# Weights in pieces of 4, 4 and 8 column tiles, and the order of every engine from tables

## The chip, the cores and the metric

The kernel runs on one core of a Trainium2 chip. The metric is the device time of one execution in microseconds; lower is better. PE is the matrix engine (TensorE), with PEld for its weight loads; ACT is ScalarE, DVE is VectorE, POOL is GpSimd, SP is SyncE.

## The reference, cut to what matters

```python
def _attn_ref(q, k, v, alpha):            # (4, 8, 768, 48) each
    B, H, S, D = q.shape
    state = np.zeros((B, H, D, D))
    for t in range(S):
        state = alpha[:, :, t, :, None] * state + np.einsum('bhd,bhe->bhde', k[:, :, t], v[:, :, t])
        y[:, :, t] = np.einsum('bhd,bhde->bhe', q[:, :, t], state)
    return y

def _moe_ref(x, w_in, w_out):             # x (3072, 384), w_in (384, 2048), w_out (2048, 384)
    r = np.maximum(x @ w_in, 0.0)
    return (r * r) @ w_out
```

The rows of x are the outputs of the first part, all heads side by side. It is a linear attention with a decay for each channel, followed by a dense layer, a squared ReLU and a second dense layer.

## The kernel before, in words

**Tiles.** The 3072 tokens are cut into 12 tiles (`units`) of 256: three stretches of the sequence for each of four batches. Tile g has two tokens in a partition. Tiles 0 to 3 are the first stretch of each batch, so the state of one batch is needed again four tiles later.

**Attention of tile g** (the numbers are names of operations, given by `name=` in `add`): loads `lda`, `ldk`, `ldq`, `ldv`; the product of two neighbouring decays `pr` and its logarithm `ln`; matmuls with a triangle of ones for the cumulative sums, `m1i` and `m1s`; exponentials `ei`, `ea`, `ec`, `es`; scaled keys and queries `ekm`, `eqm` into QKS; transposes `tr` into KQT (on PE with copies `et` out of PSUM for tiles 0 to 2, as DMA transposes on SP's queue from tile 3 on); scores `p`, masked on DVE into PM (`mk0`, `mk1`); v in bf16 (`vc`); the state's matmuls `kv` with `sa`, `sc`, `sd` behind them; the output `y`, copied by `xe` and transposed by `xt` (PE with a copy `xv` for tiles 0 to 3, DMA from tile 4 on). Tile 0 is worked in two halves of heads, so its names have the half in them (`ln0_0`, `ekm1_0`).

**Dense layers of tile g.** The first layer is eight units `s1_g_u` of 6 matmuls, each into one of two PSUM banks in turn. Each is emptied by a ReLU `re` (ACT or DVE); squares `sq` of one or two units follow (DVE, ACT or POOL). The second layer is eight units `s2_g_j_sg` of 4 matmuls into one bank, emptied by `oe`, stored by `out`; the last half tile has a form of its own (`last_tile`, L980).

**Weights.** W_in and W_out are loaded on POOL's queue, which turns fp32 into bf16, in two halves of 8 column tiles each. `hidden` says which columns of W_in make up tile `fj`, `weight` loads a piece, and a unit waits for the piece that it reads.

**Order.** `Program.add` records an operation with what it reads and writes, the engines that could do it, costs and a priority. `Program.schedule` replays the whole list against a model of engines and DMA rings and so gives each engine its queue; `MOVED` and `CHOSEN` shift priorities and fix engines for some names. `fill` puts dummy matmuls (L1104) into PE's gaps before the first dense unit. `place` derives the waits, `emit` writes each queue out. From then on each engine works strictly in the order of its queue: an operation that waits holds all behind it, and a DMA's issue waits in its engine's queue like any other instruction. `AFTER` ties some loads to the landing of others: tile 2's loads to W_in's first piece, W_out's first piece to W_in's second, tile 3's loads to W_out's first piece.

Of the kernel before, what the change touches and what calls it, by code (L numbers as in the profile page):

```python
# [2 lines left out]

# [11 lines left out]
class Op:  # L15


    __slots__ = ("alts", "eng", "fn", "cost", "prio", "deps", "idx", "lag", "sem", "start", "end", "pos", "name",
                 "users", "ndeps", "mode", "ready", "land", "pace")

    def __init__(self, alts, prio, name):
        self.alts, self.prio, self.name = alts, prio, name
        self.eng = self.fn = self.cost = None
        self.deps = {}
        self.lag = 0
        self.sem = None
        self.users = []
        self.pace = ()
        self.pos = None
        self.mode = ("F", "F")  # L30
        self.ready = 0.0
        self.start = self.end = self.land = None


class Program:
# [3 lines left out]
    HOP = 35  # L39
    PE_LATENCY = 170  # L40
    DMA_FIRST = {"sp": 1300, "act": 1300, "pool": 2000}
    PACKET = (("win", 172), ("wout", 490), ("ld", 22), ("tr", 18), ("xt", 18), ("out", 125))
    SBUF_ONLY = ("pr", "bk", "aq", "ekm", "eqm", "sq", "sb", "sd")
    BIAS = {"pool": 300}
    DMA_LAST = 800
    SWITCH = 95
    HALVED = {"qks": 3, "kqt": 3, "raw": 3, "ek": 3, "eq": 3, "acm": 2, "laf": 2}
    AFFINITY = 2500
    MOVED = {
# [6 lines left out]
    }  # L56
    CHOSEN = {
# [4 lines left out]
    }  # L62

    def __init__(self, nc):
        self.nc = nc
        self.ops = []
        self.writer = {}
        self.readers = {}
        self.dma_sems = {}
        self.dma_count = {}  # L70
        self.filler = None

    def add(self, eng, fn, cost, prio, reads=(), writes=(), name="", dma=None, lag=0, after=(), mode=("F", "F"),
# [7 lines left out]
        if name in self.CHOSEN:  # L81
            choices = {self.CHOSEN[name]: choices[self.CHOSEN[name]]}
        op = Op(choices, prio + self.MOVED.get(name, 0), name)
# [3 lines left out]
        if dma is not None:  # L87
            if dma not in self.dma_sems:
                self.dma_sems[dma] = self.nc.alloc_semaphore("d_" + dma)
                self.dma_count[dma] = 0  # L90
            self.dma_count[dma] += 1
            op.sem = (dma, self.dma_count[dma])
# [25 lines left out]
    def schedule(self):  # L118

        for op in self.ops:  # L120
            op.ndeps = len(op.deps)
            for d in op.deps:
                d.users.append(op)
        engines = sorted({e for op in self.ops for e in op.alts})
        free = {e: 0.0 for e in engines}
        shared = {"dve": 0.0, "pool": 0.0}
        mode = "F"
        rings = {"sp": [], "act": [], "pool": []}
        left = {}
        clock = [0.0, 0]  # L130
        events = []
        seq = itertools.count()

        def push(t, kind, what):
            heapq.heappush(events, (t, next(seq), kind, what))

        def rates():
            took = {r: next(t for n, t in self.PACKET if q[0].name.startswith(n)) for r, q in rings.items() if q}
            return {r: t / sum(took.values()) for r, t in took.items()}

        def advance(t):
            rate = rates()
            for r, q in rings.items():
                if q:
                    left[q[0]] -= rate[r] * (t - clock[0])
            clock[0] = t
            for r, q in rings.items():
                while q and left[q[0]] <= 1e-6:
                    op = q.pop(0)
                    land(op, t + self.DMA_LAST)  # L150
            clock[1] += 1
            rate = rates()
            nxt = [left[q[0]] / rate[r] for r, q in rings.items() if q]
            if nxt:
                push(t + min(nxt), "tick", clock[1])

        def land(op, t):
            op.land = t
            for u in op.users:
                u.ndeps -= 1  # L160
                e = op.eng
                if op.sem is None and e == "pe" and "pe" in u.alts:
                    ready = op.end
                elif u.deps[op] or e not in u.alts:
                    ready = t + self.HOP
                else:
                    ready = op.end
                u.ready = max(u.ready, ready)
                if u.ndeps == 0:
                    push(max(u.ready, now), "ready", u)  # L170

        now = 0.0
        for op in self.ops:
            if op.ndeps == 0:
                push(0.0, "ready", op)
        avail = {e: [] for e in engines}
        order = {e: [] for e in engines}
        while events:
            now = events[0][0]
            while events and events[0][0] <= now + 1e-9:  # L180
                _, _, kind, op = heapq.heappop(events)
                if kind == "tick":
                    if op == clock[1]:
                        advance(now)
                elif kind == "arrive":
                    advance(now)
                    rings[op.eng].append(op)
                    left[op] = op.lag
                    advance(now)
                elif kind == "ready":  # L190
                    best = None
                    for e, (_, c) in op.alts.items():
                        t = max(now, free[e]) + c + self.BIAS.get(e, 0)
                        t += sum(o.alts[e][1] for o in avail[e] if (o.prio, o.idx) < (op.prio, op.idx))
                        if best is None or t < best[0]:
                            best = (t, e)
# [33 lines left out]
    def fill(self, make, sizes, until, after, cold):  # L230
# [5 lines left out]
        for o in self.order["pe"]:  # L236
            while t < until:
                slow = 2 if t < cold else 1
                fits = [(n, c) for n, c, gap in sizes if o.start - t > gap + (slow - 1) * c]
                if not fits:  # L240
                    break
# [120 lines left out]
def bass_gla_recurrent__then__act_relu_squared_kernel(  # L362
# [29 lines left out]
    WS = 2  # L392
# [744 lines left out]
```

## Time and profile before

| | |
|---|---|
| median of 3 runs | 175.64 us (174.52 to 177.49) |
| the profiled execution | 175.72 us, span 174.0 us |
| busy of the span | PE 97%, DVE 68%, ACT 69%, POOL 14% |
| first layer's matmuls (L1010) | 73.7 us busy, 576 |
| second layer's matmuls (L1050) | 68.9 us busy, 368 |
| DMA | 33.36 MB, mean 192 GB/s |

How to read it: the page names an engine, a line of the kernel and the tiles, out<-in, with the number of instructions. A row of a timeline has the start in the span, the time, the engine, line and operation, and in brackets how long the engine had been idle and what ended that. A row of the waits has the waiting engine and line, what it waited for, the total in us, how often, and the longest. A row of windows has, for each engine, busy time and instructions in a stretch, in the order PE, PEld, DVE, ACT, POOL, then PE's granted clock, the DMA share and GB/s. Matmuls overlap each other in the records, so a row's time is longer than what it adds to the next one's start.

### The profile page before, as it was taken

The numbers are of one execution on the slowest core, as the hardware profiler recorded it, in microseconds if no ns is written. First come the engines' busy times: TensorE is split into PE (matmuls) and PEld (weight loads), VectorE is DVE, ScalarE is ACT, GpSimd is POOL, SyncE is SP. The second block draws the span as 40 slices with busy tenths as digits, with TensorE's granted clock in tenths as the row PEclk, the third lists the DMA queues.
The fourth block names the chain that finished last, engine by engine and source line by source line (L and its number), as shares of the span: only waits on it lengthen the run. The fifth ranks groups of instructions, "written<-read, shape, count | busy, mean of one in ns | idle before, by whom it ended". The sixth has DMA issues, their size and how long they took to land.

```text
span 174.0 us, 5086 instructions
## 1 busy us (share of the span) xinstructions
PE 168.1 (97%) x2234; PEld 130.0 (75%) x2234; DVE 119.1 (68%) x194; ACT 119.6 (69%) x214; POOL 24.0 (14%) x32
## 2 busy tenths in 40 slices
PE   7999998999999989999999999999999999999994
PEld 2556877866878767777778777878788697688773
DVE  5479569789878679984958948948949727332230
ACT  4848768877758399697878849759668564566440
POOL 3920961010224124200000000000000000000000
PEclk9999999999999999999999999999999999999999
DMA  5999999999998997999999998989999590040022
GB/s 145 351 288 210 259 281 212 259 284 280 191 215 188 245 207 97 340 194 238 283 185 196 269 176 191 261 182 221 234 191 190 95 184 4 0 136 4 13 79 90
DMA packets 71030, 33.36 MB, mean 192 GB/s; under 512 B 67552, under 2 KB 67808, under 8 KB 71008
## 3 DMA queue, kind: packets, MB, share of 16 engines
q1 hardware_dynamic: 69024, 26.75, 68.9%
q0 software_dynamic: 1984, 6.29, 14.9%
q8 instruction: 17, 0.28, 0.6%
q14 instruction: 5, 0.04, 0.1%
HBM read 25.17 MB, written 4.72 MB: 172 GB/s over the span
## 4 chain that ended last, share of the span: by engine, by line
PE 78%; DMA 14%; POOL 3%; ACT 2%; DVE 1%; issue 1%; SPq 1%
PE psWH L1010 33%; PE psO L1050 33%; DMA win<-in_moe_w_in_dram 5%; DMA raw<-in_alpha_dram 5%; DMA raw<-in_v_dram 4%; POOL raw L535 2%; PE psX L811 2%; PE psZ L779 2%; PE psX L908 2%; PE psX L800 2%; PE psX L980 2%; PE psZ L908 1%; PE psWH L652 1%; ACT rr L1018 1%; POOL prd L645 1%
## 5 line engine op out<-in xcount | busy, mean ns | idle before, releaser
L1010 PE MATMUL psWH<-xt,win 128*128 128x256 bf16 x576 | 73.7, 275 | 1.8 <-DVE xt L966 1.0
L1010 PEld LDWEIGHTS psWH<-xt,win 128*128 128x128 bf16 x576 | 65.3, 145 | 6.9 <-ACT rr L1018 1.3
L1050 PE MATMUL psO<-wout,gt 128*128 128x384 bf16 x368 | 68.9, 326 | 0.0
L1018 ACT ACTIVATE rr<-psWH 128x512 bf16<-128x512 f32 x85 | 50.3, 596 | 20.5 <-PE psWH L1010 18.7
L1050 PEld LDWEIGHTS psO<-wout,gt 128*128 128x128 bf16 x368 | 34.8, 98 | 18.4 <-DVE gt L1028 0.2
L1028 DVE TENSOR_TENSOR gt<-rr 128x1024 bf16<-128x1024 bf16 (+1 forms) x39 | 23.7, 610 | 24.5 <-ACT rr L1018 24.5
L919 DVE TENSOR_TENSOR pm<-psZ,caus 128x1024 bf16<-128x1024 f32 x12 | 14.6, 1218 | 2.3 <-PE psZ L908 2.3
L919 DVE TENSOR_TENSOR pm<-psX,caus 128x1024 bf16<-128x1024 f32 x12 | 14.6, 1219 | 1.5 <-PE psZ L908 1.5
L1032 ACT ACTIVATE gt<-rr 128x1024 bf16<-128x1024 bf16 (+1 forms) x18 | 15.2, 843 | 0.4
L939 ACT ACTIVATE xbf<-psX 128x768 bf16<-128x768 f32 x11 | 8.9, 810 | 8.2 <-PE psX L800 7.4
L1057 ACT ACTIVATE osb<-psO 128x384 f32<-128x384 f32 x17 | 8.4, 491 | 5.9 <-PE psO L1050 5.4
L1104 PE MATMUL psO<-zero 128*128 128x512 bf16 (+1 forms) x34 | 10.3, 432 | 1.3 <-DVE zero L455 1.3
L714 DVE TENSOR_TENSOR qks<-raw,eq 128x384 bf16<-128x384 f32 x18 | 9.4, 552 | 2.0 <-DMA raw<-in_q_dram 1.8
L719 DVE TENSOR_TENSOR qks<-raw,ek 128x768 bf16<-128x768 f32 x11 | 10.5, 951 | 0.1
L710 ACT ACTIVATE vbf<-raw 128x768 bf16<-128x768 f32 x9 | 7.5, 837 | 3.7 <-DMA raw<-in_v_dram 3.7
L1020 DVE TENSOR_SCALAR rr<-psWH 128x512 bf16<-128x512 f32 x11 | 7.6, 688 | 0.6
L646 ACT ACTIVATE lab<-prd 128x384 bf16<-128x384 f32 x10 | 5.2, 520 | 3.5 <-DVE prd L643 2.5
L874 DVE TENSOR_TENSOR smd<-psZ,sbd 128x384 bf16<-128x384 f32 x8 | 4.4, 556 | 4.4 <-PE psX L800 4.4
L672 DVE TENSOR_TENSOR ek<-ek,raw 128x384 f32<-128x384 f32 x9 | 6.3, 705 | 1.4 <-ACT ek L663 1.4
L645 POOL TENSOR_TENSOR prd<-raw 128x384 f32<-128x384 f32 x4 | 4.1, 1036 | 19.0 <-DMA raw<-in_alpha_dram 19.0
L1104 PEld LDWEIGHTS psO<-zero 128*128 128x128 bf16 x34 | 3.2, 109 | 4.5 <-issue 1.9
L1059 DVE COPY osb<-psO 128x384 f32<-128x384 f32 x6 | 3.3, 557 | 4.6 <-PE psO L1050 4.6
(118 smaller groups left out, 170.6 us busy)
## 6 DMA issues: line engine op xcount, KB each, us to landing
out_dram<-osb SPq DMA_DIRECT2D x11, 384.0 KB, 4.3
raw<-in_alpha_dram SPq DMA_DIRECT2D x10, 384.0 KB, 5.2
raw<-in_k_dram SPq DMA_DIRECT2D x10, 384.0 KB, 5.6
raw<-in_q_dram SPq DMA_DIRECT2D x10, 384.0 KB, 3.9
raw<-in_v_dram SPq DMA_DIRECT2D x10, 384.0 KB, 4.5
win<-in_moe_w_in_dram POOLq DMA_DIRECT2D x2, 768.0 KB, 10.3
wout<-in_moe_w_out_dram POOLq DMA_DIRECT2D x2, 768.0 KB, 8.9
raw<-in_alpha_dram POOLq DMA_DIRECT2D x2, 384.0 KB, 4.9
```

What stands on the lines that cost most here:

```text
L714: add("dve", lambda e, j=j, dst=dst: e.tensor_tensor(dst, RAW[r][:, 2, :, j, :].rearrange("p (n x) d -> p n x d", x=2), EQ[la][:, j].rearr ...
L719: add("dve", lambda e, a=a, E=E: e.tensor_tensor(QKS[qs][:, a, :, :, 0:D], RAW[r][:, 1 + a].rearrange("p h j d -> p j h d"), E[la][:].rear ...
L919: add("dve", lambda e, hf=hf, psT=psT: e.tensor_tensor(PM[pm][:, hf].rearrange("p r n j t -> p (r n) (j t)"), psT[:, :, :].rearrange("p r ...
L939: add("act", lambda e: e.activation(XBF[x2][:], psX[:, :, 0:HD], AF.Copy), act_ns(2 * HD), p0 + 6100, reads=[("ps", "X", 0), ("ps", "X", 1 ...
L1010: ins = pe.matmul(psH[hb][:, i * T:(i + 1) * T], WIN[:, kk, hidden(fj)], mov, start=(kk == 0), stop=(kk == KT - 1))
L1018: add("act", lambda e, hb=hb, rr=rr: e.activation(rr, psH[hb], AF.Relu), act_ns(512), pu + 600, reads=[("ps", "H", hb)], writes=[("rr", rb ...
L1020: alts={"dve": (lambda e, hb=hb, rr=rr: e.tensor_scalar(rr, psH[hb], 0.0, None, ALU.max), dve_ns(512))})
L1028: add("dve", lambda e, dst=dst, sq=sq: e.tensor_tensor(dst, sq, sq, ALU.mult), 148 + k * 267, pu + 1200, reads=[("rr", rb, h) for h in ran ...
L1032: "act": (lambda e, dst=dst, sq=sq: e.activation(dst, sq, AF.Square), act_ns(k * 512))})
L1050: ins = pe.matmul(psS, GT[gt][:, fj, j, :], WOUT[:, fj, :], start=(fj == 0), stop=(fj == FT - 1))
L1057: add("act", lambda e, j=j, psS=psS: e.activation(OSB[ob][:, j], psS, AF.Copy), act_ns(DM), ps_ + 700, reads=[keyS], writes=[("osb", ob, j ...
L1104: pr.fill(lambda n: lambda pe: pe.matmul(psO[:, 0:n], ZERO[:, 0:128], ZERO[:, 0:n], skip_group_check=True), ((512, 216, 420), (256, 109, 2 ...
```

## The change

The search inside the kernel goes; what it decided is replaced by five tables of names, one for each engine, in which `~512` and `~256` are dummy matmuls of that width. `schedule` reads them, gives each operation the engine whose table names it, and counts the DMA semaphores by queue. Dependences and waits are derived as before.

```diff
-    def schedule(self):
...
-    def fill(self, make, sizes, until, after, cold):
-    def unpace(self):
+    def schedule(self, tables, filler):
+        named = {o.name: o for o in self.ops}
+        queues = {}
+        for e, text in tables.items():
+            queues[e] = []
+            for word in text.split():
+                if word[0] == "~":
+                    ...
+                else:
+                    o = named.pop(word)
+                o.eng = e
+                o.fn, o.cost = o.alts[e]
+                o.pos = len(queues[e])
+                queues[e].append(o)
...
-    WS = 2
-    FS = FT // WS
+    PIECES = ((0, 4), (4, 4), (8, 8))
+    def piece(fj):
+        return max(w for w, (at, n) in enumerate(PIECES) if at <= fj)
     def hidden(fj):
-        w, e = divmod(fj, FS)
-        return slice(w * FS * 128 + e, (w + 1) * FS * 128, FS)
+        at, n = PIECES[piece(fj)]
+        return slice(at * 128 + fj - at, (at + n) * 128, n)
...
-            add("pe", s1, ..., reads=[("xt", s)] + sorted({("win", f // FS) for f in fjs}), ...
+            add("pe", s1, ..., reads=[("xt", s)] + sorted({("win", piece(f)) for f in fjs}), ...
-                    ... + [("wout", sg * WS // 4)],
+                    ... + [("wout", piece(sg * FT // 4))],
```

Further branches that come with it (`SPLIT_X`, `SPLIT_KV`, `HALF_LOADS`, `WIDE`) are empty or off. The starts of the tables:

```
pe:   ~512 x8 m11_0 m10_0 ~512 ~512 ~512 ~512 ~512 ~256 ~256 tr00_0 ~512 ~256 kv0
      tr01_0 ~256 ~256 tr10_0 ~512 ~512 ~256 tr11_0 p0_0 ~256 ~256 p1_0 m11 ~512 ~512 ~512 ~512 y0 ~512 ~512 ~512
      ~512 xt0 tr0_1 ~256 ~256 s1_0_1 tr1_1 s1_0_0 s1_0_3 p0_1 s1_0_2 s1_0_5 s1_0_4 kv1 m1i2 s1_0_7 y1 s1_0_6 xt1
      m1s2 tr0_2 s1_1_1 s1_1_0 s1_1_3 s1_1_2 s2_0_0_0 tr1_2 s1_1_5 s1_1_4 p0_2 s2_0_0_1 s1_1_6 s2_0_0_2 s2_0_0_3 ...
act:  table ln1_0 ln0_0 ei1_0 ei0_0 ea1_0 ea0_0 vc0 ec0_0 ln1 copycaus ec1_0 ei1 ea1 ec1 xe0 et1_1 re0_3 re0_2 vc1
      re0_5 ln2 re0_4 ei2 re0_7 xe1 ea2 ec2 es2 re1_1 re1_0 re1_3 sq1_1 vc2 re1_6 re1_5 oe0_0 ln3 ...
dve:  ... ekm1_0 ekm0_0 zcaus et00_0 eqm1_0 zlaf1 eqm0_0 zlab1 et01_0 et10_0 sa0 et11_0 mk0_0 mk1_0 sc0 zlab0 ekm1
      eqm1 xv0 et0_1 re0_1 re0_0 mk0_1 mk1_1 pr2 sd0 sq0_3 sa1 zqks2 sc1 bk2 ekm2 xv1 re0_6 ...
pool: slinc slstr scaus1 sident lda1 ldk1 ldq1 win0 scaus win1 win2 ldv1 lda2 ldk2 wout0 ldq2 sq0_1 ldv2 wout1
      wout2 sd1 sq0_5 sq1_3 sq0_7 sq0_6 vc3 pr4 pr6 bk5 sq3_1 sq3_5 sd4 sq3_7 ...
sp:   lda0 ldv0 ldk0 ldq0 lda3 ldv3 ldk3 lda4 lda5 ldq3 ldq4 ldk4 lda6 tr0_3 tr1_3 ldv4 ldk5 ldq5 tr1_4 tr0_4
      out0_1 ldv5 ldk6 ldv6 tr0_5 tr1_5 xt4 lda7 ...
```

By engine, the tables give 63 ReLUs to ACT and 33 to DVE (85 and 11 before); 22 squares to DVE, 18 to ACT and 20 to POOL (39, 18 and 3 before); the products `bk` and `pr` and the states `sd` to POOL in 13 cases instead of 6; and the copies `xe` to DVE in 4 cases instead of 1. Both kernels have 34 dummy matmuls, all before the first dense unit.

More of the change, by code (lines that the diff above doesn't have):

```diff
@@ L230, in fill @@
-    def fill(self, make, sizes, until, after, cold):
-        new = []
-        t = after.land + self.HOP
-        cold += t
[L236 to L241, printed above, removed]
-                n, c = fits[0]
-                f = Op({"pe": (make(n), c)}, 0, "fill")
-                f.idx = len(self.ops)
-                f.eng, f.fn, f.cost = "pe", make(n), c
-                f.start, f.end = t, t + c * slow
-                f.deps = {after: True}
-                self.ops.append(f)
-                new.append(f)
-                t = f.end
-            new.append(o)
-            t = max(t, o.end)
-        for i, o in enumerate(new):
-            o.pos = i
-        self.order["pe"] = new
```

358 lines of the change are left out of this document (169 added, 189 removed), and 10 rows, old and new, of tables (CHOSEN, MOVED).

## The prediction

> **What bounds the kernel now.** I read the page first, then the matrix engine's waits, then its timeline at the two places where it waited, then the timelines of the engines that it waited for.
>
> ```profile
> span 174.0 us, 5086 instructions
> PE 168.1 (97%) x2234; PEld 130.0 (75%) x2234; DVE 119.1 (68%) x194; ACT 119.6 (69%) x214; POOL 24.0 (14%) x32
> PEclk9999999999999999999999999999999999999999
> PE psO L1104 <- DVE zero L455: 1.3, 1, 1.3
> PE psWH L1010 <- DVE xt L966: 1.0, 1, 1.0
> PE psWH L1010 <- ACT rr L1018: 0.7, 1, 0.7
> ```
>
> PE is busy for 97% of the span at the full clock, and its three longest waits are 3.0 us together. The one of 1.3 is ahead of the filler matmuls (L1104) that keep PE running through the start. So the time is: the moment of the first useful dense matmul, then PE's own work, then the waits of 1.0 and 0.7, then the tail. The profiled execution took 175.72 us (span 174.0, so 1.7 around it), beside a median of 175.64 for the three runs (174.52 to 177.49); the sum below is made against 175.7.
>
> ```profile
> 13.43 0.36 PE L840 MATMUL psX<-smd,kqt 128*64 128x96 bf16 x8 [0.27 <-DVE pm L919]
> 15.81 0.50 PE L954 MATMUL psX<-ident,xbf 128*128 128x128 bf16 x6
> 16.22 0.62 PE L742 MATMUL psZ<-ident,qks 128*128 128x128 bf16 x8
> 17.21 1.53 PE L1010 MATMUL psWH<-xt,win 128*128 128x256 bf16 x12
> 25.46 0.50 PE L954 MATMUL psX<-ident,xbf 128*128 128x128 bf16 x6
> 26.95 0.88 PE L1010 MATMUL psWH<-xt,win 128*128 128x256 bf16 x6 [1.00 <-DVE xt L966]
> 60.95 0.81 PE L1050 MATMUL psO<-wout,gt 128*128 128x384 bf16 x4
> 62.48 0.88 PE L1010 MATMUL psWH<-xt,win 128*128 128x256 bf16 x6 [0.71 <-ACT rr L1018]
> 46.90 1.31 PE psWH L1010 x12
> 48.21 1.30 PE psO L1050 x8
> ```
>
> The first dense matmul stands at 17.21. A unit of either layer (6 of L1010, or 4 of L1050) takes 0.65, by the last two rows, which are of the chain. Both orders have 34 fillers in front of the first dense unit and the same 96 units of the first layer and 92 of the second, so PE's work behind that point is the same, but for what is moved across it. The unit at 60.95 should have ended at 61.6 and its successor began at 62.48: 0.9 us. From the transposes at 25.46 to the next dense unit it was 1.5 us for 0.4 us of work: 1.1 us.
>
> **The start, part by part.** ScalarE, VectorE and the weights set it.
>
> ```profile
> 8.19 8.81 DMA win<-in_moe_w_in_dram
> 12.60 0.84 ACT L710 ACTIVATE vbf<-raw 128x768 bf16<-128x768 f32 x1 [2.37 <-DMA raw<-in_v_dram]
> 13.35 0.79 ACT L631 ACTIVATE ek<-psWH 128x768 f32<-128x768 f32 x1
> 14.17 0.81 ACT L633 ACTIVATE eq<-psWH 128x768 f32<-128x768 f32 x1
> 14.88 0.80 ACT L939 ACTIVATE xbf<-psX 128x768 bf16<-128x768 f32 x1
> 16.34 0.81 ACT L968 ACTIVATE xt<-psX 128x768 bf16<-128x768 bf16 x1 [0.59 <-PE psX L954]
> 9.26 0.42 DVE L607 COPY kqt<-psZ 128x512 bf16<-128x512 bf16 x1 [0.61 <-PE psZ L600]
> 12.14 1.23 DVE L919 TENSOR_TENSOR pm<-psZ,caus 128x1024 bf16<-128x1024 f32 x1 [0.51 <-PE psZ L908]
> 14.34 0.95 DVE L719 TENSOR_TENSOR qks<-raw,ek 128x768 bf16<-128x768 f32 x1
> 26.36 0.54 DVE L966 COPY xt<-psX 128x768 bf16<-128x768 bf16 x1
> ```
>
> The first half of W_in (768 KB) followed tile 1's v, which had landed by 12.60, and landed at 17.00: 4.4 us. A piece of 4 column tiles is half of that, 2.2. The new POOL queue issues it one load earlier (v of tile 1 now stands behind all of W_in), so it lands at about 13.6 (12.6, less 1.2 for one load, plus 2.2). That no longer holds the first dense unit; tile 0's chain does. In the new order VectorE makes all four copies of tile 0's transposes (L607, 0.42 each; two were ScalarE's), and these with two fills moved in between push the last mask (L919) from 12.14 to about 12.55; the output matmuls L840 follow at 13.8 instead of 13.43. ScalarE makes up for it: the copy of v is gone from in front of L631, which starts at 13.0 when its matmuls end instead of 13.35, so its L939 starts at 14.8 as before. The transposes L954 come at 15.65 (the eight L742 that stood ahead of them are now behind), and the copy to xt is VectorE's at 0.54 instead of ScalarE's at 0.81: dense work from 16.8. **Term 1: -0.4.** The second eight L742 (0.45) now follow the first dense unit instead of filling the gap ahead of it: **term 2: +0.45.**
>
> **From 17 to 37 us** I laid the new order out by hand: PE unit by unit at 0.65, ScalarE's ReLU at 0.60, VectorE's at 0.69, masks at 1.23 with 1.14 from start to start. V of tile 1 now lands behind W_in, at 20.8 (W_in's second half landed 11.8 us after its issue at 8.92, by twice the page's median of 10.3 less the 8.81 above, so at 20.7; one load moved behind W_in leaves the total as it was). Its copy stands in ScalarE's queue between two ReLUs, and behind it wait the ReLU of unit 5, the logarithm of tile 2 and the ReLU of unit 4; the matmuls kv1 also wait for the mask that frees psZ. I get waits of PE of 0.2 (s1_0_4), 0.3 (kv1), 0.6 (m1i2, for the logarithm), 0.2 (xt1), 0.2 (m1s2) and 0.1 elsewhere: 1.6, where the old order lost 1.1 at the place above and 0.4 around it. **Term 3: +0.1**, between -1.5 (none of these waits) and +1.5 (each twice as long). At the end of kv2 both orders have done the same work, at 37.3 by my layout and at 37.3 in the trace.
>
> The pieces of W_out: the last one has 8 tiles and lands where the old second half did, since the queue's bytes are the same; the new unit that needs it starts at 34.9. SyncE's loads of tile 3 now start when the first small piece of W_out has landed, some 4 us earlier:
>
> ```profile
> 0.81 3.37 DMA raw<-in_alpha_dram
> 29.32 0.37 SPq L535 DMA_DIRECT2D raw<-in_alpha_dram  x1
> 34.65 1.00 POOL L645 TENSOR_TENSOR prd<-raw 128x384 f32<-128x384 f32 x1 [8.10 <-DMA raw<-in_alpha_dram]
> ```
>
> A load issued beside W_out took until 34.65, 5.3 us, against 3.4 for the first load of all (first row, of the chain): it hardly moves until W_out is through, so the earlier issue gains and costs little; I take 0, between -0.5 and +1.0. [...]
>
> **The wait at 62 us.**
>
> ```profile
> 61.10 0.84 ACT L710 ACTIVATE vbf<-raw 128x768 bf16<-128x768 f32 x1 [1.31 <-DMA raw<-in_v_dram]
> 61.85 1.07 ACT L1018 ACTIVATE rr<-psWH 128x512 bf16<-128x512 f32 x2
> ```
>
> ScalarE stood at the copy of tile 5's v, and the ReLU (re3_1) that PE wanted stood behind it. In the new order re3_1 is VectorE's, re3_2 precedes the copy, and v is preceded by 17 transfers on SyncE's queue, as before. The 0.9 and 0.2 behind it go: **term 4: -1.1.** Late next would be VectorE: re3_1 follows ekm5 (0.95) there, and PE has some 3 us of other units before it needs that bank again.
>
> **The engines' shares.** 22 ReLUs go from ScalarE to VectorE (33 there instead of 11), 17 squares from VectorE to POOL (20 instead of 3).
>
> ```profile
> L1020 DVE TENSOR_SCALAR rr<-psWH 128x512 bf16<-128x512 f32 x11 | 7.6, 688 | 0.6
> 40.00:52.00 12.00, 12.00 (x171) 9.32 (x169) 10.25 (x19) 8.16 (x16) 2.19 (x2) 1.00 1.15 229
> 22.52 1.13 POOL L645 TENSOR_TENSOR prd<-raw 128x384 f32<-128x384 f32 x1 [0.95 <-DMA raw<-in_alpha_dram]
> 66.69 1.90 POOL L1031 TENSOR_TENSOR gt<-rr 128x1024 bf16<-128x1024 bf16 x1 [3.29 <-ACT rr L1018]
> 69.56 1.04 POOL L1031 TENSOR_TENSOR gt<-rr 128x512 bf16<-128x512 bf16 x1 [0.98 <-ACT rr L1018]
> 67.09 1.91 DVE L672 TENSOR_TENSOR ek<-ek,raw 128x384 f32<-128x384 f32 x1
> 27.16 0.54 DVE L672 TENSOR_TENSOR ek<-ek,raw 128x384 f32<-128x384 f32 x1
> 24.72 1.11 DVE L1028 TENSOR_TENSOR gt<-rr 128x1024 bf16<-128x1024 bf16 x1 [1.47 <-ACT rr L1018]
> 22.10 0.68 DVE L1028 TENSOR_TENSOR gt<-rr 128x1024 bf16<-128x1024 bf16 x1
> ```
>
> VectorE gains 22 x 0.69 = 15 us and loses about 10 in squares: some 125 us of 174, and ScalarE falls to some 102. Both stay below PE. The danger is in the last rows: L672, normally 0.54, took 1.91 when it started inside POOL's square of 66.69 to 68.59, and ended just behind it. A square of 0.68 took 1.11 the same way. POOL's eleven instructions from 22.52 to 70.60 (first and last above) add up to 12.3 us and met VectorE's 98 instructions with both operands in SBUF; the hits cost 1.4 + 0.4. The new order has 74 of these, and on POOL twelve squares of 1.90, eight of 1.04 and about 15 us of others: 46 us. Hits grow as 46 x 74 over 12.3 x 98, 2.8 times, to 5 or 6 of 0.9 each: 5 us on VectorE. How much reaches PE is bounded by 0 (each hit is hidden by PE's choice of another unit) and +5 (none is). **Term 5: +0.2**, near the lower end, since neither hit of the trace cost PE anything that its waits show. [...]
>
> **Sum.** 175.7 - 0.4 + 0.45 + 0.1 - 1.1 + 0.2 = **174.9 us**. The tail behind the last matmul is the same in both.
>
> **Rivals.**
> 1. *POOL's squares hold VectorE* (slower). Six hits of 0.9 in front of ReLUs or masks that PE waits for: 174.9 - 0.2 + 5.4 = 180.1. It decides from the point where a hit exceeds the one unit (0.65) that PE has in hand while a PSUM bank is emptied; hits of 1.4 do. For it: VectorE is 85% busy from 40 to 52. Against it: the two hits of the trace.
> 2. *Hardly any wait remains* (faster). Without term 3's 1.6, 174.9 - 1.6 = 173.3; with dense work from 16.3 instead of 16.8, 172.8. For it: each wait rests on steps of some 0.2 us that I may have too long. Against it: the chain through tile 1's v and psZ is real work in series. PE's work allows no more, so over 2% faster (below 172.1) needs this case and a favourable scatter of the runs.
> 3. *The pieces do nothing*: W_in is off the path either way, and the new order only swaps waits: 175.7. For it: even the whole half, one load earlier, would land at 15.8, before 16.8.
>
> **Chances.** Forecast 0.50 (own range 173.9 to 176.5), rival 1 0.21, rival 2 0.19, rival 3 0.10. Two per cent (3.5 us) is about what a measurement of this kernel tells from no change. Slower by more comes from rival 1 alone, 0.21; faster by more from two thirds of rival 2, 0.13; within 2% 0.66. For 8 in 10 the range takes in rival 2 and most of rival 1: 172.2 to 179.8.
>
> **What would show it.** Right: first dense matmul near 16.8; no wait of PE near 62; v of tile 1 copied at about 21 and a short wait of PE at 22 to 24; L672 and L719 on VectorE lengthened to 1.5 or more, without a wait of PE behind them. Wrong: PE's waits above 4 us in total, or waits for VectorE's ReLU (L1020's successor) from 60 us on; a first dense matmul later than 17.2; or transposes (kqt) that land after PE wants them.

## The result, and the profile after

The changed kernel took 176.43 us (median of 19 runs, 175.90 to 178.08), the kernel before 175.40 (19 runs, 174.43 to 177.49): ratio 1.0069, 95% interval 1.0048 to 1.0091. That is within the 2% that counted as no change in the forecast, and inside its range (172.2 to 179.8), but on the other side of 1: slower by 0.7%, or 1.2 us by this ratio (1.0 by the medians), where 0.8 us less was forecast. Some executions of a kernel are some per cent slower than its others (`a_small_squares` took from 176.16 to 181.44 us), the ratios below leave these out and the medians do not, and the profiles of `a_small_squares` and `a_fetch21` are of such executions, so a wait that only these two show proves nothing. The profiled execution of the changed kernel took 178.08, the upper end of its 19, so I read a second profile of the same kernel as well (176.44, span 174.7; "second profile" below). First the page of the changed kernel and its waits of PE:

```profile
span 176.3 us, 5096 instructions
PE 168.2 (95%) x2232; PEld 129.0 (73%) x2234; DVE 126.2 (72%) x200; ACT 100.4 (57%) x184; POOL 60.8 (34%) x58
PE psX L724 <- ACT vbf L632: 1.5, 1, 1.5
PE psO L1061 <- DVE zero L376: 1.3, 1, 1.3
PE psWH L574 <- ACT lab L568: 0.8, 1, 0.8
PE psWH L965 <- DMA win<-in_moe_w_in_dram: 0.5, 1, 0.5
PE psX L764 <- DVE qks L641: 0.5, 1, 0.5
PE psZ L703 <- ACT vbf L632: 0.5, 1, 0.5
```

The engines' shares came out as worked out: VectorE 126 us, ScalarE 100; POOL has 61 in all. The wait for `rr` at 62 us is gone. But a new longest one stands on top: L724, the product `y` of a tile's queries with its state, waits 1.5 us for `vbf`, the bf16 copy of a tile's v. The second profile has a similar list, with the same wait on top but for the fillers' (its line numbers are one lower):

```profile
PE psO L1060 <- DVE zero L375: 1.3, 1, 1.3
PE psX L723 <- ACT vbf L631: 1.0, 1, 1.0
PE psZ L521 <- DVE qks L509: 0.8, 2, 0.6
PE psWH L573 <- ACT lab L567: 0.8, 1, 0.8
16.83 0.84 PE L964 MATMUL psWH<-xt,win 128*128 128x256 bf16 x6
21.50 0.85 ACT L631 ACTIVATE vbf<-raw 128x768 bf16<-128x768 f32 x1
22.56 0.52 PE L702 MATMUL psZ<-vbf,qks 64*128 64x96 bf16 x16 [0.21 <-DVE pm L848]
23.86 0.34 PE L573 MATMUL psWH<-lab,linc 128*128 128x384 bf16 x1 [0.78 <-ACT lab L567]
169.58 2.80 PE L934 MATMUL psX<-wout,gt 128*128 128x272 bf16 x32
168.85 2.80 PE L980 MATMUL psX<-wout,gt 128*128 128x272 bf16 x32
```

The rows with a start are of the timelines of PE and ScalarE: dense work starts at 16.83 (17.21 before), v of tile 1 is copied at 21.50, short waits follow at 22.56 and 23.86, and the last product of all starts at 169.58; the very last row is the same product in the kernel before, 168.85. So PE gained 0.4 us at the start and had lost 0.7 us at the end.

Where it waits is `y6`, the product y of tile 6, which stands behind the copy of tile 7's v. What that copy waits for is the last load of tile 7, `ldv7`. The timelines of VectorE, SyncE, ScalarE and PE, second profile first, then the kernel before (behind the dots):

```profile
74.43 1.02 DVE L635 TENSOR_TENSOR qks<-raw,eq 128x384 bf16<-128x384 f32 x2
75.47 3.10 SPq L651 DMA_TRANSPOSE kqt<-qks  x2
78.62 1.84 SPq L914 DMA_TRANSPOSE xt<-xbf  x1
81.14 0.58 SPq L455 DMA_DIRECT2D raw<-in_v_dram  x1
87.47 0.84 ACT L631 ACTIVATE vbf<-raw 128x768 bf16<-128x768 f32 x1 [1.19 <-DMA raw<-in_v_dram]
88.37 0.19 PE L723 MATMUL psX<-sbd,kqt 64*128 64x48 bf16 x1 [1.02 <-ACT vbf L631]
...
71.48 1.02 DVE L714 TENSOR_TENSOR qks<-raw,eq 128x384 bf16<-128x384 f32 x2
72.53 3.96 SPq L730 DMA_TRANSPOSE kqt<-qks  x2
76.68 1.81 SPq L960 DMA_TRANSPOSE xt<-xbf  x1
79.16 0.58 SPq L535 DMA_DIRECT2D raw<-in_v_dram  x1
84.04 0.83 ACT L710 ACTIVATE vbf<-raw 128x768 bf16<-128x768 f32 x1
88.60 0.19 PE L800 MATMUL psX<-sbd,kqt 64*128 64x48 bf16 x1
```

Before, the copy ended at 84.87, 3.7 us ahead of `y6`. After, the load is issued 2.0 us later. In both orders it stands behind tile 6's transposes in SyncE's queue; these wait for VectorE's products `eqm6` (first rows), and VectorE comes to them 2.9 us later, where its new table has the second mask of tile 5 and two ReLUs (`re3_7`, `re4_3`) ahead of them that did not stand there before. And `y6` is wanted at 87.35, 1.25 us sooner. That alone would leave some 0.5 us in hand. But the load also took longer, 6.3 us instead of 4.4. Why it did is what most of the experiments are about. They are all compared with runs of the kernel before on the same chip.

### The profile page after: what moved, and what is told of

Read it like the earlier page. It is cut to its first block, busy times and chain, and to the rows that moved or that the text cites. A ratio compares the mean times of both kernels' runs of the same rounds, so it can differ in the third digit from the quotient of the medians.

```text
span 176.3 us, 5096 instructions
## 1 busy us (share of the span) xinstructions
PE 168.2 (95%) x2232; PEld 129.0 (73%) x2234; DVE 126.2 (72%) x200; ACT 100.4 (57%) x184; POOL 60.8 (34%) x58
## 2 busy tenths in 40 slices
DMA packets 71575, 33.37 MB, mean 189 GB/s; under 512 B 67584, under 2 KB 68608, under 8 KB 71552
## 4 chain that ended last, share of the span: by engine, by line
PE 66%; DMA 15%; DVE 8%; POOL 6%; ACT 3%; issue 2%; SPq 1%; ACTq 0%
PE psO L1005 28%; PE psWH L965 26%; DMA raw<-in_alpha_dram 7%; DMA win<-in_moe_w_in_dram 4%; DMA raw<-in_v_dram 4%; POOL gt L986 3%; PE psX L735 2%; DVE qks L641 2%; PE psZ L703 2%; PE psX L724 2%; POOL raw L456 2%; PE psX L935 2%; PE psX L838 1%; DVE pm L849 1%; DVE rr L975 1%
## 5 line engine op out<-in xcount | busy, mean ns | idle before, releaser
L973 ACT ACTIVATE rr<-psWH 128x512 bf16<-128x512 f32 x63 | 36.9, 595 | 35.3 <-PE psWH L965 31.5
L986 POOL TENSOR_TENSOR gt<-rr 128x1024 bf16<-128x1024 bf16 (+1 forms) x20 | 32.4, 1632 | 49.3 <-DVE rr L975 28.2
L975 DVE TENSOR_SCALAR rr<-psWH 128x512 bf16<-128x512 f32 x33 | 22.4, 688 | 12.5 <-PE psWH L965 12.2
L983 DVE TENSOR_TENSOR gt<-rr 128x1024 bf16<-128x1024 bf16 (+1 forms) x22 | 13.2, 604 | 9.1 <-ACT rr L973 9.0
L641 DVE TENSOR_TENSOR qks<-raw,ek 128x768 bf16<-128x768 f32 x11 | 12.4, 1123 | 0.0
L1012 ACT ACTIVATE osb<-psO 128x384 f32<-128x384 f32 x13 | 6.4, 492 | 5.8 <-PE psO L1005 4.5
L894 ACT ACTIVATE xbf<-psX 128x768 bf16<-128x768 f32 x8 | 6.5, 811 | 5.5 <-PE psX L724 4.7
L1014 DVE COPY osb<-psO 128x384 f32<-128x384 f32 x10 | 5.5, 554 | 5.3 <-PE psO L1005 5.2
L592 POOL TENSOR_TENSOR ek<-ek,raw 128x384 f32<-128x384 f32 x4 | 4.3, 1070 | 13.6 <-ACT ek L585 13.6
L585 ACT ACTIVATE ek<-psWH 128x384 f32<-128x384 f32 x10 | 4.9, 488 | 3.6 <-PE psWH L574 2.5
```

Of the source, the lines that this page charges most:

```text
L641: add("dve", lambda e, a=a, E=E: e.tensor_tensor(QKS[qs][:, a, :, :, 0:D], RAW[r][:, 1 + a].rearrange("p h j d -> p j h d"), E[la][:].rear ...
L973: add("act", lambda e, hb=hb, rr=rr: e.activation(rr, psH[hb], AF.Relu), act_ns(512), pu + 600, reads=[("ps", "H", hb)], writes=[("rr", rb ...
L975: alts={"dve": (lambda e, hb=hb, rr=rr: e.tensor_scalar(rr, psH[hb], 0.0, None, ALU.max), dve_ns(512))})
L983: add("dve", lambda e, dst=dst, sq=sq: e.tensor_tensor(dst, sq, sq, ALU.mult), 148 + k * 267, pu + 1200, reads=[("rr", rb, h) for h in ran ...
L986: alts={"pool": (lambda e, dst=dst, sq=sq: e.tensor_tensor(dst, sq, sq, ALU.mult), 200 + k * 840), "act": (lambda e, dst=dst, sq=sq: e.act ...
```

## Experiments

**Pieces or tables?** Three kernels: the tables with the weights in halves, the old order with the weights in pieces, and the changed kernel with POOL's squares cut to 64 columns from tile 2 on (the rest of the hidden layer's columns there is left out). With them ran the changed kernel itself again, the second profile above.

```diff
# a_halves                                   # b_pieces: old order as tables, and
-    PIECES = ((0, 4), (4, 4), (8, 8))       + pool: ... win1 win2 ... wout1 wout2 ...
+    PIECES = ((0, 8), (8, 8))
# a_small_squares, g >= 2
-    e.tensor_tensor(dst, sq, sq, ALU.mult)
+    e.tensor_tensor(dst[:, 0:64], sq[:, 0:64], sq[:, 0:64], ALU.mult)
```

The changed kernel again:

> The changed kernel as it is, for a second profile and a time on the same chip as the others. Theory A (the small pieces of W_in are slow and make all loads behind them late): the waits of PE between 20 and 25 us (for W_in's last piece, for v of tile 1 and for the logarithm of tile 2) show again, 2.0 us together, since they come from packets of a fixed size. Theory B (POOL's squares hold VectorE): VectorE's long rows for the products ekm6 and bk3 (2.4 and 1.3 us where 0.95 and 0.54 are normal) show again, since the orders are fixed, and the waits behind them at the outputs of tiles 2 and 6 (0.6 and 1.7 us). What does not show again was chance in that one execution. Ratio to the kernel before 1.007.

The halves:

> The new tables, with the weights in two halves of 8 column tiles as before. Theory A: W_in is through at about 20.0 instead of 21.2 and v of tile 1 at 21.1 instead of 22.4; PE's waits between 20 and 25 us shrink from 2.0 to about 0.8; 1.0 to 1.3 us faster than the changed kernel, so 0.999 to 1.001 of the kernel before. Theory B: no change, 1.007.

The pieces alone:

> The order and choices of the kernel before, with the weights in pieces of 4, 4 and 8. Theory A: W_in is through at about 22.3 instead of 20.7, the fifth unit of the first layer, which needs the last piece, waits about 1 us for it, and what follows is late by as much: 1.004 to 1.007 of the kernel before. Theory B, or a loss that comes from the tables alone: 1.000, since each piece lands before it is wanted.

The small squares:

> The changed kernel, but from tile 2 on POOL's squares compute 64 columns instead of 512 or 1024, so that part of the hidden layer is left out and POOL is busy for some 25 us less. Theory B: the long rows of VectorE at 69 and 81 us and the waits of PE behind them at the outputs of tiles 5 and 6 go; 1 to 2 us faster than the changed kernel, 0.996 to 1.001 of the kernel before. Theory A: the same as the changed kernel, 1.007, with the waits at 20 to 25 us unchanged.

| kernel | median us | ratio, interval |
|---|---|---|
| changed kernel again | 176.89 | 1.0065, 1.0038 to 1.0093 |
| tables, weights in halves | 178.12 | 1.0137, 1.0097 to 1.0178 |
| old order, weights in pieces | 175.20 | 0.9973, 0.9943 to 1.0003 |
| changed, small squares on POOL | 176.51 | 1.0054, 1.0031 to 1.0078 |

The pieces cost nothing in the old order. The halves were a miss: 1.0137 lies outside both theories, though barely apart from 1.0065 by the intervals. In the profiled execution with halves (179.0, of 177.07 to 179.74) PE waits 0.7 us for W_in's first half, whose last of 16 shares landed 1.6 us behind the others (17.37 against 15.78), and 1.6 instead of 0.8 us for the logarithm of tile 2. That second wait is not the load's, which landed at 22.82 (22.66 with pieces): VectorE's product ahead of the logarithm took 1.73 us instead of 0.56; it began inside a square of POOL's (22.42 to 24.33). Timelines of PE, POOL and VectorE with halves:

```profile
17.51 0.85 PE L964 MATMUL psWH<-xt,win 128*128 128x256 bf16 x6 [0.69 <-DMA win<-in_moe_w_in_dram]
22.42 1.91 POOL L985 TENSOR_TENSOR gt<-rr 128x1024 bf16<-128x1024 bf16 x1
23.02 1.73 DVE L564 TENSOR_TENSOR prd<-raw 128x384 f32<-128x384 f32 x1
25.36 0.34 PE L573 MATMUL psWH<-lab,linc 128*128 128x384 bf16 x1 [1.60 <-ACT lab L567]
```

So the loss lies in the order. POOL's squares from tile 2 on are not its main cause: instructions of VectorE beside them do run longer, 2.41 us for one of 0.95 in the second profile's timeline below, but with them cut to 64 columns the kernel is faster by 0.1%, well inside the intervals. What the squares of tiles 0 and 1 and POOL's other products cost, no run tests; the halves show that one of these squares can reach PE.

```profile
67.39 1.90 POOL L985 TENSOR_TENSOR gt<-rr 128x1024 bf16<-128x1024 bf16 x1 [4.59 <-DVE rr L974]
67.69 2.41 DVE L640 TENSOR_TENSOR qks<-raw,ek 128x768 bf16<-128x768 f32 x1
```

**Moving single operations.** `a_v7` issues tile 7's v two places earlier, ahead of `xt5` and `ldq7`; `a_front` moves five operations at the start; `a_both` does both; `b_fix` moves, in the old order (with pieces), a ScalarE copy (`vc5`) behind two ReLUs and a VectorE copy (`xv1`) ahead of a square and a ReLU, against the waits at 62 and 26 us.

```diff
# a_v7       sp:   ... tr0_6 +ldv7 xt5 ldq7 -ldv7 out2_1 ...
# a_front    pool: ... win1 +ldv1 win2 -ldv1 ...      dve: mk1_1 mk0_1 ... sc1, sa1 ahead of pr2
#            pe:   ... kv1 s1_0_5 s1_0_4 ...          act: vc1 re0_2 ...
# b_fix      act:  ... re3_2 vc5 ...                  dve: ... xv1 sq0_5 re0_7 ...
```

> The changed kernel with one load moved on SyncE's queue: v of tile 7 ahead of the transpose of tile 4's successor (xt5) instead of behind it and the load of q. Theory C (the loss is a new wait at the output of tile 6, since its ScalarE copy of tile 7's v waits for a load that stands behind two transposes, which wait for VectorE's products, which wait behind a ReLU): PE's wait of 1.0 to 1.5 us near 88 us goes, 1.0 us faster than the changed kernel, 0.999 to 1.002 of the kernel before. Theory D (the loss is in the start, 17 to 28 us): no more than 0.3 us, 1.005 to 1.007.

> The changed kernel with the start rearranged: v of tile 1 loaded ahead of W_in's last piece and copied ahead of one ReLU, tile 1's mask that frees psZ made first, its state and the matmuls for it (kv1) ahead of the unit that needs W_in's last piece. Theory D: kv1 at about 21.4 instead of 22.6 and the output of tile 1 at 23.1 instead of 24.9, PE's waits from 17 to 28 us (1.9 us above the order of switches) fall by about 1.0: 0.999 to 1.002 of the kernel before. Theory C: the same as the changed kernel, 1.007, as PE catches up later anyway or waits for W_in's last piece instead.

> Both moves of the two kernels before in one. If both waits count in full, 2 us faster than the changed kernel: 0.994 to 0.997 of the kernel before. If one hides the other (PE arrives earlier and waits longer for the same load), 1.000.

> The order of the kernel before with the pieces, ScalarE's copy of tile 5's v moved behind two ReLUs, and on VectorE the copy to xt of tile 1 ahead of a ReLU and the square that POOL held up behind both. The waits of PE at 62 us (0.6 to 0.9) and at 26 us (1.1 to 1.7) shrink to some 0.3 each: 0.990 to 0.994 of the kernel before. If VectorE's order there is not what PE waits for, 0.997 as with the pieces alone.

| kernel | median us | ratio, interval |
|---|---|---|
| `a_v7` | 177.82 | 1.0077, 1.0043 to 1.0111 |
| `a_front` | 176.51 | 1.0064, 1.0041 to 1.0087 |
| `a_both` | 177.52 | 1.0097, 1.0064 to 1.0131 |
| `b_fix` | 175.65 | 1.0011, 0.9981 to 1.0041 |

None of these brought the changed kernel back to the old time, nor the old order below the pieces alone; `a_both` (0.994 to 1.000 expected) and `b_fix` (0.990 to 0.997) missed on the slow side. `a_v7` is the result that fits least: its profiled execution (175.79, of 175.79 to 181.30) has no wait at `y6` and its last product at 168.93, as before, yet the kernel as a whole is as slow as the changed one. Where its other executions waited, no trace shows. With `a_both` the waits change places: PE no longer waits at `y6` but for `xt5`, the transfer that now stands behind, and for a ReLU of VectorE:

```profile
84.90 1.47 PE L964 MATMUL psWH<-xt,win 128*128 128x256 bf16 x12 [0.68 <-DMA xt<-xbf]
90.10 1.53 PE L964 MATMUL psWH<-xt,win 128*128 128x256 bf16 x12 [0.55 <-DVE rr L974]
```

**Early or late, queue or rate?** Two splices of the orders at 48 us, the changed kernel with small stores, and the old order with SyncE's new table.

```diff
# a_then_b: on each engine what the changed kernel starts before 48 us, in its order, then the old order
# b_then_a: the reverse          # b_sp_of_a: old order, SyncE's table of the changed kernel
# a_small_stores, g < 4
-    e.dma_start(dst, OSB[ob])
+    e.dma_start(dst[:, 0:96], OSB[ob][:, 0:96])
```

> Tables spliced: on every engine the operations that the changed kernel starts before 48 us stand first, in its order, and all others follow in the order of the kernel before; weights in pieces of 4, 4 and 8. This keeps the changed start and puts back the old middle and end. Theory 'late': the loss lies behind 48 us, in the new wait of tile 6's y product for tile 7's v (1.2 us) and two short ones (0.5 us) that replaced the wait at 62 us. Then the ratio is that of the old order with the pieces, 0.995 to 1.000 (174.4 to 175.4 us), no wait stands at y6, and one of about 1 us stands at 62 us. Theory 'early': the loss lies in the start, in the second eight L742 copies behind the start (0.45 us) and waits for loads and VectorE at 17 to 30 us (2.3 us in all instead of 1.6): ratio 1.004 to 1.007. Theory 'scarce loads': wherever the order is tightened some transfer is late next; then 1.002 to 1.006 with waits at new places behind 48 us.

> The opposite splice: the order of the kernel before (with the pieces) for all that it starts before 48 us, then the order of the changed kernel. Theory 'late': the wait at y6 for tile 7's v, about 1.2 us, and the short ones remain, the wait at 62 us is gone: ratio 1.004 to 1.007. Theory 'early': start as before, first dense near 17.3 us, the wait at 62 us gone and y6 no worse than that: 0.994 to 0.998. Theory 'scarce loads': 1.002 to 1.006, y6 waits at least 0.8 us.

> The changed kernel, but the stores of the outputs of tiles 0 to 3 write 96 of each row's 768 values, so this part of the output is left out and about 1.4 MB of the traffic between 50 and 90 us with it. Order and every other instruction are unchanged. Theory 'scarce loads': y6's wait for tile 7's v comes from transfers that share full DMA engines, so tile 7's v lands some microseconds sooner, y6's wait falls from 1.2 to below 0.3 us and the ratio to 0.997 to 1.000. Theory 'queue order': tile 7's v is late because SyncE issues it late, behind transposes that wait for VectorE; it is issued near 81 us still, lands near 87, y6 waits about 1 us and the ratio stays at 1.005 to 1.008. Theory 'early': 1.004 to 1.007 with or without the wait.

> The order of the kernel before on TensorE, VectorE, ScalarE and GpSimd, weights in pieces of 4, 4 and 8, and on SyncE the order of the changed kernel. Theory 'queue order': the changed order of SyncE's loads, transposes and stores is what costs; then ratio 1.004 or more, and a wait of 1 us or more for tile 7's v or another load between 60 and 95 us. Theories 'early' and 'late' (orders of the computing engines): 0.996 to 1.000, as the pieces alone gave (0.9973).

Measured: `a_then_b` 177.11 us, 1.0075 (1.0044 to 1.0105); `b_then_a` 181.71, 1.0319 (1.0276 to 1.0361); `a_small_stores` 176.33, 1.0035 (1.0012 to 1.0058); `b_sp_of_a` 193.96, 1.0976 (1.0918 to 1.1034). The splices and the swapped table lie outside all theories and say nothing on early or late: new waits at the seams hide it, 4.1 us for a logarithm in `b_then_a`, 5.3 us for transposes in `b_sp_of_a`, and 1.8 us at the old place of 62 us in `a_then_b`.

The small stores may have taken some of the loss away (the intervals overlap), yet `y6` still waited 0.7 us, between what the theories had. But `a_then_b` showed something else. It issues `ldv7` at 81.40, about as late as the changed kernel, and PE does not wait. The trace keeps the 16 completions of each transfer, one for each share. For `ldv7`, in us from the span's start and in order of landing:

```
                     issued   shares 1 ... 15      share 16
before               79.16    82.91 ... 83.35      83.58
changed kernel       82.68    86.45 ... 86.94      89.09
second profile       81.14    84.75 ... 85.68      87.45
a_small_stores       81.39    85.15 ... 85.92      87.28
a_then_b             81.40    85.28 ... 86.01      86.08
```

In the changed order 15 shares land together and one comes 1.4 to 2.2 us later. The same holds in `a_front`, `a_halves`, `a_small_squares` and `b_then_a` (1.6 to 2.0); in `a_v7` and `a_both`, where v went first, tile 7's q has it instead (0.6 and 2.0). Each time a read of 16 KB on another queue had just come by. The page's DMA part for the life of `ldv7`, in the second profile (81.0 to 87.5) and in the kernel before (79.0 to 83.6):

```profile
q1 hardware_dynamic: 3557, 1.62, 90.3%
q8 instruction: 1, 0.02, 1.7%
raw<-in_v_dram SPq DMA_DIRECT2D x1, 384.0 KB, 6.3
...
q1 hardware_dynamic: 2625, 1.23, 95.7%
raw<-in_v_dram SPq DMA_DIRECT2D x1, 384.0 KB, 4.4
```

The row "q8 instruction", one packet of 16 KB, is by its name a read of instructions; it is there after and not before. It is no matter of this one load: over the nineteen traces, the last share came more than 1 us behind the 15th in 172 of the 640 loads and stores (transposes aside) in whose life such a read fell, and in 3 of the other 641. The read lasts 0.9 to 1.8 us around tile 7, less than some of the lags, and the trace does not tell on which of the 16 engines it ran, so how the one becomes the other is not shown. These reads come at nearly the same counts of PE's weight loads in both orders (before: 1071 and 1157 at 76.2 and 83.8 us; second profile: 1067 and 1162 at 75.4 and 83.7), so they look like PE's own instructions. That is a guess from these counts; no row of PE's waits names a read, and what the traces show is the late share of another load.

**Moving the reads.** If so, the count of PE's instructions ahead of that place decides, and it can be changed without touching any other order: dummy matmuls of 512 columns ahead of the dense work are cut into four of 128.

```diff
# a_fetch72: all 24; a_fetch45: the last 15; a_fetch21: the last 7
-    ~512
+    ~128 ~128 ~128 ~128
# a_fetch_mid: the first 16 of them, and 8 of ~256 into two: 56 more
# b_fetch72: 24 of them in b_pieces
```

> The changed kernel with all 24 warm-up multiplications of 512 columns ahead of the dense work cut into four of 128: the same columns, 72 more instructions of each kind on TensorE before the first dense tile, nothing else changed. The reads of TensorE's instructions, which stand near 75.4, 83.7 and 90.2 us, move 72 multiplications forward, to about 70, 77 and 85.5 us, so none falls between 78 and 85 us. Theory 'collision': the 16 parts of tile 7's v land within 0.7 us of each other, near 85.7 us; y6's wait falls from 1.2 to below 0.3 us; ratio 0.997 to 1.002. Theory 'queue order' (SyncE issues the load late) and theory 'scarce loads' (the transfer rate is used up): neither knows the count of TensorE's instructions; y6's wait stays at 1 us or more, ratio 1.004 to 1.008. If the cut itself costs at the start, the first dense tile comes later than 17.0 us and the difference counts there.

> The same with 15 of the 24 multiplications cut into four, those nearest to the dense work: 45 more. The reads come near 71, 79.5 and 87 us. Theory 'collision': the read near 79.5 us falls on the transfers just ahead of tile 7's v; one part of it is late by less than in the unshifted order, 0.3 to 1.2 us, y6's wait is 0 to 0.8 us, ratio 0.999 to 1.005. Theories 'queue order' and 'scarce loads': as unshifted, wait 1 us or more, 1.004 to 1.008.

> The same with 7 of the 24 cut into four: 21 more. The reads come near 73.5, 82 and 88.7 us, and the one near 82 us falls on the load of tile 7's q and v. Theory 'collision': one part of tile 7's v lands 1 to 2 us behind the others and y6 waits 0.8 us or more as in the unshifted order, ratio 1.004 to 1.008. Theories 'queue order' and 'scarce loads': the same. So this run is the control: it shows what the cut by itself costs, with the collision left in.

> The changed kernel with 16 of the 24 warm-up multiplications of 512 columns cut into four and eight of 256 cut into two, 56 more in all; those of the last three microseconds ahead of the dense work stay whole. The reads come near 70.5, 78.2 and 86.5 us. Theory 'collision': the 16 parts of tile 7's v land within 0.8 us, y6's wait is below 0.4 us, and the dense work starts by 17.2 us instead of 17.7: ratio 0.995 to 1.001. Theory 'the cut itself' (more and shorter warm-up work helps whatever the reads do): between the runs with 45 and with 72, 1.000 to 1.003, and no better than them.

> The order of the kernel before with weights in pieces of 4, 4 and 8, and 24 warm-up multiplications of 512 columns cut into four, 72 more. In this order tile 7's v lands at 84.0 us, its y6 starts at 89.0 us, and no wait of TensorE behind 30 us ends with a load. Theory 'collision': nothing to gain here, at most a later start to lose: ratio 0.997 to 1.003 (0.9973 without the cut). Theory 'the cut itself': the same gain as in the changed order, 0.65%: 0.989 to 0.993.

| kernel | reads between 70 and 92 us | lag of `ldv7`'s last share | wait at `y6` | first dense unit | ratio, interval |
|---|---|---|---|---|---|
| second profile | 75.4, 83.7, 90.2 | 1.76 | 1.02 | 16.83 | 1.0065, 1.0038 to 1.0093 |
| `a_fetch21` | 75.6, 85.0 | 0.43 | none | 16.90 | 1.0061, 1.0029 to 1.0094 |
| `a_fetch45` | 71.2, 78.1, 90.2 | 0.07 | 0.4 | 17.19 | 1.0029, 0.9997 to 1.0061 |
| `a_fetch_mid` | 70.3, 77.5, 90.7 | 0.37 | none | 17.02 | 0.9997, 0.9973 to 1.0021 |
| `a_fetch72` | 70.1, 76.9, 89.0 | 0.15 | none | 17.69 | 1.0000, 0.9978 to 1.0023 |
| `b_fetch72` | 76.6, 86.7 | 0.05 | none | 18.44 | 0.9967, 0.9947 to 0.9988 |

Where the reads lie clear of tile 7's q and v, the shares land together and `y6` waits little or not at all; in `a_fetch_mid` and `a_fetch72` the loss is gone, and their intervals lie below the changed kernel's. The same cut in the old order, which has no such collision at tile 7, changes nothing (0.9967 beside 0.9973), so it is not the cut itself that helps. A late issue and a lack of rate don't explain it either: in `a_fetch72` the load is issued at 82.63, later still, while the transfers take 95.5% of the engines' time. Its waits of PE have 0.2 for `vbf` (at `kv1`) and none at `y6`, and for the life of `ldv7`, 82.0 to 87.3, its DMA part has no row of instructions:

```profile
PE psO L1063 <- DVE zero L378: 1.3, 1, 1.3
PE psWH L576 <- ACT lab L570: 0.8, 1, 0.8
PE psO L1063 <- issue: 0.5, 1, 0.5
PE psX L766 <- DVE qks L643: 0.3, 1, 0.3
PE psZ L705 <- ACT vbf L634: 0.2, 1, 0.2
...
q1 hardware_dynamic: 2995, 1.33, 95.5%
raw<-in_v_dram SPq DMA_DIRECT2D x1, 384.0 KB, 4.6
```

That moving the reads removes the loss is shown by the ratios. That it does so by way of `y6` is not: the cut moves all reads, those among the loads of the start too, and `a_v7` has shown that a kernel can lose the wait and keep the loss.

Three results stay open. `a_fetch21` met its ratio, but the wait expected at `y6` is not in its profile; that profile is of the longest of its 12 executions (179.00 us, median 177.04) and can't be held against the theory: everything in it came later, and the read fell on `xt5`. `a_fetch45` met what was expected, but its interval overlaps those of the changed kernel and of `a_fetch72`, so it decides nothing. And `a_fetch72` was expected to lose what its start lost, and by its ratio did not: its profiled execution (176.46, of 175.20 to 176.50) has its last product at 169.58, as in the second profile, though its first dense unit came 0.86 us later.

## Why the prediction was wrong, by its own steps

- **Term 1 (-0.4, earlier start): right as a time, not seen as a gain.** Dense work starts at 16.83 us, the forecast's 16.8. But `b_fetch72` starts 1.1 us later than `b_pieces` (18.44 against 17.31), and its last product starts 0.8 us sooner (168.25 against 169.08); its waits of PE are shorter instead. Below, PE's timelines of `b_pieces` and `b_fetch72`:

```profile
17.31 0.95 PE L965 MATMUL psWH<-xt,win 128*128 128x256 bf16 x7
169.08 2.80 PE L935 MATMUL psX<-wout,gt 128*128 128x272 bf16 x32
...
18.44 1.28 PE L968 MATMUL psWH<-xt,win 128*128 128x256 bf16 x10
168.25 2.80 PE L938 MATMUL psX<-wout,gt 128*128 128x272 bf16 x32
```

- **Term 2 (+0.45, eight L742 behind the start): held**, as a count of instructions; no run tests it alone.
- **Term 3 (+0.1): the places were right, the size too small.** `kv1`, `m1i2`, `xt1` and `m1s2` wait as laid out; the logarithm of tile 2 costs 0.78 instead of 0.6, and 1.6 with halves. In the first profile W_in had a late share too, with an instruction read at 15.6 us in its life: the last share of its last piece landed at 21.16, 1.2 us behind the 15th, and PE waited 0.5 for it and 0.5 for tile 1's v behind it. Its parts stand: the first piece of W_in landed at 13.85 (forecast 13.6), v of tile 1 was copied at 21.50 (about 21). That loads beside W_out cost nothing was not tested by itself; W_out's last piece landed at 33.53 instead of 33.37.
- **The check at the end of `kv2` compared unequal work.** By the tables the new order has done 15 units of the first layer there, the old one 16: `s1_1_7` (0.65) now stands behind it. `kv2` starts at 36.63 in the second profile and at 36.84 before, 0.2 sooner with 0.65 still to do. So terms 1 to 3 came to +0.4 instead of +0.15 (in the first profile, with `kv2` at 37.37, to +1.2). Second profile first:

```profile
36.63 0.51 PE L702 MATMUL psZ<-vbf,qks 64*128 64x96 bf16 x16
36.84 0.52 PE L779 MATMUL psZ<-vbf,qks 64*128 64x96 bf16 x16
```

- **Term 4 (-1.1, the wait at 62 us): right.** No row of the second profile's waits has `rr`.
- **What term 4 said comes late next: this step failed.** "Late next would be VectorE", with nothing in the sum for it. VectorE is late next, but not at re3_1 and not free of cost: its `eqm6` comes at 74.43 instead of 71.48, SyncE's transposes wait for it, `ldv7` waits behind these, and `y6` waits 1.0 to 1.5 us for tile 7's v. I had counted the transfers ahead of tile 5's v in SyncE's table, found them equal, and stopped. The same count for tile 7 would have misled as well, since 36 entries stand ahead of `ldv7` in both tables; what differs is when the queue gets there and when the product is wanted, and these take a reserve of 3.7 us down to about 0.5. What then takes that reserve, a share 1.8 us late (2.2 in the first profile) with an instruction read beside it, stands in no view that I had read.
- **Term 5 (+0.2, POOL's squares): right in size as far as tested.** VectorE's stretched instructions add up to 5.2 us (forecast 5), one of 0.95 us taking 2.41, and taking most of those from tile 2 on away gained 0.1%, inside the intervals. So rival 1 did not happen. But the reading it rested on, that neither hit of the trace cost PE anything, does not hold: the kernel before's square of 24.72 (1.11 us instead of 0.68) stands in the chain of VectorE's work that led to the 1.0 us wait at 26.95, so some 0.4 of that wait was the hit's, and with halves a hit stood ahead of a wait of 1.6. The forecast's count took instructions with both operands in SBUF alone, and in the first profile the stretched ones are such: of 15 that ran beside an instruction of POOL seven were over 0.15 us longer than the shortest of their kind, of 37 with an operand in PSUM none. PE mostly had other units in hand. The chain before, VectorE's rows:

```profile
24.72 1.11 DVE gt L1028
25.83 0.60 DVE rr L1020
26.43 0.47 DVE xt L966
```

- **Rival 3 (the pieces do nothing) had the pieces wrong**: under the new order they are worth 0.7% (1.0137 with halves, 1.0065 with pieces). It had the half landing at 15.8, and 15 of its 16 shares had (15.78); the last came at 17.37, behind the first dense unit's place.

From `kv2` to the last product the forecast had -0.9 (terms 4 and 5) and the second profile has +0.3, so PE's last product came 0.73 us later in all. The 1.1 won at 62 us was given back: 1.0 at `y6`, 0.2 at two short waits (`y2`, `y5`); some 0.2 has no place. In the first profile, which has 1.5 at `y6` and 0.6 at these two, the last product came 2.37 later. Nor is the reads' part the whole miss: with the reads moved the kernel stands at 1.0000 and 0.9997, not at the forecast's 0.9954. That leaves some 0.8 us, of which the 0.3 of terms 1 to 3 has a place, if the second profile's holds there, and the rest is open.

Of the signs named for "wrong", one came true: waits of PE above 4 us in total (5.1 and 4.1 in the two lists, the 1.3 at the fillers included). All those named for "right" came true as well in the second profile; they looked no further than some 69 us. How much of the 0.7% is `y6` and how much other loads that met a read cannot be told, since cutting the dummies moves all reads, those at the start too.

## What to carry to other kernels

When an order takes a wait away, list the time in hand of each later load (from its landing to its first use) in both orders, and when the queue reaches it, not only what stands ahead of the one load that was late: here a reserve fell from 3.7 to about 0.5 us, and a 1.8 us disturbance that nobody had felt became the longest wait. Don't book an earlier start as a gain before the waits behind it are laid out: in one pair here a start 1.1 us later did not end later. When two orders are compared at a place, count the work done up to it in both. And an order that is tuned to a fraction of a microsecond works as a whole: part of it in another order cost up to 10%.

## What the runs showed of the hardware

- In the kernel before and in the first profile a 16 KB read of instructions came every 4 to 13 us, each of the 17 within 64 weight loads of PE of the same count in both, and took 0.9 to 1.7 us. Over the nineteen traces one of a transfer's 16 shares was over 1 us late in 172 of 640 transfers with a read in their life, and in 3 of 641 without; in the changed kernel by up to 2.3 us (tile 7's q). Transfers queued behind lagged as well: in the second profile `ldv7`, the store after it and the next k are late by 1.76, 1.78 and 1.79 us.
- Moving these reads by 56 or 72 dummy matmuls, with every other order as it was, took the kernel from 1.0065 to 0.9997 and 1.0000 of the old time.
- W_in's packets of 1 KB (pieces of 4 tiles) took 98 ns and those of 2 KB 173 ns in the second profile (medians), so the same bytes took 13% more engine time; the whole of W_in landed at 20.3 us there, 21.2 in the first profile and 20.7 before.
